# Retention and a gated two-layer network in one kernel: a given TensorE order, held-back weight sums and three releases for the weight slabs

## The chip, the cores and the metric

The kernel runs on one core of a Trainium2 chip. The metric is device time in microseconds, the median of several runs. Lower is better.

## The reference

```python
# q, k, v: (8, 8, 576, 64); w_in: (512, 2048); w_out: (2048, 512)
scores = (q @ k.T) / sqrt(64)
Dmat   = where(rel >= 0, gamma[h] ** rel, 0)      # gamma = 1 - 2 ** (-5 - head)
x      = (scores * Dmat) @ v                      # then (4608, 512): token by all heads
h      = x @ w_in
g      = h * cos(h)
out    = g @ w_out                                # (4608, 512), float32
```

The first part is causal attention with a decay in place of a softmax. The second is a network of two layers on all 4608 tokens, with `h * cos(h)` between them.

## The kernel before

**Tiling.** The tokens are done in nine blocks of 512 (`NTB` is 9), numbered j. A block holds two chunks of 64 positions for four batches. Two streams of two batches each, `x` and `y` in the names, run through 18 chunks: nine for the first four batches, nine for the other four.

**Attention.** The decay is split into a factor on q, a factor on v and a running state, so that a chunk needs only its own keys and the state. `kv_tile` and `q_tile` load k, v and q through SP's queue into `stgk`, `stgv` and `stgq`, and cast or scale them into `natk`, `natv` and `qnat`. In the first tiles ("fast") ScalarE and VectorE do most of this, later GpSimd does. The tiles are then transposed, by TensorE and a copy (`tpe`, `tph`) or by a DMA (`txb`), into `kt` and `qt`. `session` then makes up to four kinds of small products of 64 by 64: q with the old state (L652), q with k (L634), the new state (L643) and, after VectorE has masked the scores into `pt` (L723), the masked scores with v (L661). ScalarE copies the result into `xt` and the state into `sbd`.

**The network.** `mlp1` multiplies `xt` with `win` (L763), four products to a group. ScalarE takes the cosine into `cb` (L771) and VectorE multiplies it into `gt` (L774). For blocks 0 to 2 a group has 256 columns, later 512. The second layer of block 0 is plain (`plain2`, L800). The others use seven products in place of eight (`wino2`, L886). This needs sums of the activations (`s`) and sums of the second weights (`wsums`, L826): six into `tw`, two that overwrite a quarter of `wout`. These overwrites may only run once `plain2` has read that part. ScalarE and VectorE drain the results into `os`, and SP's queue stores them.

**What sets the order.** `graph` lists all tasks with a priority in ns, and `Graph.run` plans them. It keeps a clock for each engine, takes the task that can start first, and among those that can start within some 40 to 60 ns the one with the smallest priority. Each engine runs its tasks in the planned order, and waits on semaphores where a producer or a buffer's last reader isn't done. Buffers come from pools (six PSUM banks `bk`, three `stgk`, three `stgv`, two `stgq` and so on). The planner models instruction fetches: `fetched` keeps a task back while the next block of 256 instructions is not there, with 6000 ns for a fetch and 3500 more for three of them. In its gaps at the start TensorE runs dummy products on a tile of ones (`warm`, L418), so that it isn't idle.

**Weights.** `win` and `wout` come in four slabs of 512 KB each, which GpSimd's queue issues (`load_w`). The first slab is issued once the first v load has landed, and the seven others once the second half of the second tile's q has landed. Two later k loads wait for two slabs of `wout` (`GATE`).

Of the kernel before, what the change touches and what calls it, by code (L numbers as in the profile page):

```python
# [29 lines left out]
class Prog:  # L30
# [9 lines left out]
    def add(self, eng, fn, r=(), w=(), sem=None, after=()):  # L40
# [4 lines left out]
        for k in w:  # L45
            readers = self.rd.get(k, [])
            deps += [d for d in readers if d.eng != eng or d.sem or sem]
            deps += self.wr.get(k, [])
# [54 lines left out]
class Buf:  # L103
    __slots__ = ("pool", "slot", "tasks", "left", "free")

    def __init__(self, pool):
        self.pool, self.slot, self.tasks, self.left, self.free = pool, None, [], 0, 0.0


class Task:  # L110
    @property
    def allocs(self):
# [3 lines left out]
                 "port", "name", "order", "late", "ops", "ni", "pre")  # L116
# [13 lines left out]
def slack(a, b):  # L130

    return Graph.SLACK if b.eng == "pe" and (a.eng == "pool" or a.dma is not None) else 0


class Graph:


    BACKLOG, FETCH, SLOW, MARGIN, SLACK, DX, DLAT = 3500, 6000, 3500, 60, 0, 1.18, 2400

    def __init__(self, pools):  # L140
        self.tasks, self.wr, self.rd = [], {}, {}
        self.pools = {p: [0.0] * n for p, n in pools.items()}
        self.fifo = {p: [] for p in pools if p not in ("bk", "s", "sn", "cb")}
        self.holder = {p: [None] * n for p, n in pools.items()}

    def add(self, eng, dur, parts, prio=None, alloc=(), dma=None, port=False, name="", late=0.0, ni=0):
        t = Task()
        t.ni, t.pre = ni, 0
# [54 lines left out]
    def run(self, dma_rate):  # L203
        self.prios()
        free = {e: 0.0 for e in ("pe", "act", "dve", "pool", "sp")}
        ready = {e: [] for e in free}
        dma_free, port_free = 0.0, {"dve": 0.0, "pool": 0.0}
        est, order, count, got, cold = {}, [], 0, [], True
        for t in self.tasks:
            est[t] = 0.0  # L210
            if not t.wait:
                ready[t.eng].append(t)
# [15 lines left out]
        def fetched(t):  # L228

            k, s = math.ceil(count / 256 - 1.754), 0  # L230
            while k >= 0 and (k + 1.754) * 256 <= count + t.ni + (self.MARGIN if t.ni > 60 else 0):
                if k < len(got):
                    s = max(s, got[k] - t.dur * ((k + 1.754) * 256 - count) / t.ni)
                elif t.ni > 60:
                    s = max(s, free["pe"] + self.FETCH - t.dur)
                k += 1
            return s

        def pick(e):
            cand = []  # L240
            for t in ready[e]:
                a = slots(t)
# [5 lines left out]
                if t.dma is not None and e != "pool":  # L248
                    s = max(s, dma_free - self.BACKLOG)
                if t.ni:  # L250
                    s = max(s, fetched(t))
                cand.append((s, t))
            if e == "pe":
                due = [t for t in ready[e] if all(any(f is not None and f <= free[e] + 1500 for f in self.pools[b.pool])
                                                  for b in t.allocs if b.pool != "bk") and sum(b.pool == "bk" for b in t.allocs) > 2 and t.prio <= free[e] + 300 and est[t] <= free[e] + 1500 and fetched(t) <= free[e] + 500]
                if due:
                    d = min(due, key=lambda t: t.prio)
                    cand = [(s, t) for s, t in cand if t is d or not any(b.pool == "bk" for b in t.allocs)]
                    mine = [s for s, t in cand if t is d]
                    if mine:  # L260
                        cand = [(s, t) for s, t in cand if t is d or s + t.dur <= mine[0] + 150]
# [7 lines left out]
        while n < len(self.tasks):  # L269
# [14 lines left out]
            if e == "pe":  # L284
                if cold and s - free[e] > 300:
                    t.pre = int((s - free[e] - 200) // 75)
                    count += 2 * t.pre
                cold = cold and t.name != "m1_0_0"
                count += 0.53
            free[e] = s + t.dur  # L290
            if t.ni:
                while (len(got) + 0.74) * 256 <= count + t.ni:
                    at = s + t.dur * max(0, (len(got) + 0.74) * 256 - count) / t.ni
                    got.append(at + self.FETCH + (self.SLOW if len(got) in (3, 10, 17) else 0))
                count += t.ni
            if t.port:
                port_free[e] = s + t.dur
            for b in t.allocs:
# [6 lines left out]
                self.holder[b.pool][i] = b  # L305
            done = s + t.dur
            if t.dma is not None:
                dma_free = max(dma_free, s + (2400 if e == "pool" else 1100)) + t.dma * self.DX
                done = dma_free + self.DLAT
# [7 lines left out]
            for o in t.succ:  # L317
                end = next(x for d, x in o.deps if d is t)
                est[o] = max(est[o], (done if t.dma is not None else s + end) + lat(t, o) + slack(t, o))
# [4 lines left out]
        self.end = max(free.values())  # L324
        return self.order


class Kernel:
# [16 lines left out]
    LEAD = 1  # L345
    NOXBAR = set(range(7))
    PERIOD, T0, T1 = 31000, 18000, 30000
# [30 lines left out]
    def build(self):  # L378
        self.graph()
        order = self.G.run(None)  # L380
# [34 lines left out]
    def warm(self, n):  # L415
        def mm(e):
            for _ in range(n):
                inst = e.matmul(ap(self.at(self.wb), 512, 0, 128, 0, [1, 128]), self.ONE.ap(), self.ONE.ap(),  # L418
# [70 lines left out]
    def kv_tile(self, x, gen, R, xbar, fast, gate=()):  # L489
# [14 lines left out]
        def casts():  # L504
# [16 lines left out]
            else:  # L521
                for b2 in range(2):
                    self.tpe(t["natk"], 512 * b2, [(b2,)], 4, t["kt"], 512 * b2, (b2,), "act")
# [14 lines left out]
    def q_tile(self, x, gen, i, xbar, fast, gate=()):  # L538
# [4 lines left out]
        for b2 in range(2):  # L543
            t = {k: Buf(k) for k in ("stgq", "qnat")}
            t["qt"] = Buf("qt" if nr > 1 else "q8")
            self.kv[x, gen, r0 // 2]["stgq"] = t["stgq"]
# [19 lines left out]
            else:  # L566
                self.tpe(t["qnat"], 0, [(y,) for y in range(nx)], 4 * nx, t["qt"], 0, (0,), "dve" if fast else "act")

    def tpe(self, src, off, rk, n, dst, doff, wk, eng):
        bk = Buf("bk")  # L570

        def mm(e):
            tb = self.at(bk).ap().bitcast(BF16)
            for c in range(n):
# [5 lines left out]
                 alloc=() if self.first else (self.wb,), name="tpe")  # L580
# [36 lines left out]
    def session(self, outs, scs, prio):  # L617
# [64 lines left out]
        def part(streams, rk, wk, after=()):  # L682
# [10 lines left out]
            t += 31 * max(map(len, streams))  # L693
# [85 lines left out]
    def store(self, j, half, os, cols=(0, DM)):  # L779
# [3 lines left out]
        for p0, n, gen, r in ([(0, 128, g0, r0)] if one else [(0, 64, g0, r0), (64, 64, g0 + 1, 0)]):  # L783
            at = ((4 * gen + 2 * half) * S + CH * r) * DM + c0
            self.one("sp", 675, lambda e, p0=p0, n=n, at=at: e.dma_start(
                bass.AP(self.out, at, [[DM, n], [S * DM, 2], [1, cn]]),
                ap(self.at(os), 1024, p0, n, c0, [512, 2], [1, cn])),
                r=[(os, c) for c in range(2) if cols[0] <= 256 * c < cols[1]],
                sem=lambda p0=p0: f"o{os.slot}_{p0}_{c0}", dma=1400 * cn / DM * n / 128)
# [21 lines left out]
    def wsums(self):  # L811
# [7 lines left out]
        for q in range(2):  # L819
            k0, k1 = q, 2 + q  # L820
            for dst, x, y, r, w in (
# [5 lines left out]
                         r=r, w=[w], port=True)  # L827

    def wino2(self, j, base, span):
# [25 lines left out]
        A, Bb, C = Buf("bk"), Buf("bk"), Buf("bk")  # L855
# [24 lines left out]
        for n, p in enumerate((1, 2, 6, 5, 7, 3, 4)):  # L880
            l, rr, keys, bank, first = spec[p]
            for q in range(2):
                def mm(e, l=l, rr=rr, bank=bank, first=first, q=q):
                    for f in range(4 * q, 4 * q + 4):
                        for tt in range(2):
                            inst = e.matmul(ap(self.at(bank), 512, 0, 128, 256 * tt, [1, 256]), l(f, tt), rr(f),  # L886
                                            start=(first and f == 0 and tt == 0), stop=True, skip_group_check=True)
                    return inst
                self.one("pe", 8 * 109, mm, ni=16, r=keys(q), w=[(bank,)], prio=base + span * (2 * n + q) / 14, name=f"P{p}_{j}")

            def view(h, c):
# [135 lines left out]
```

## Time and profile before

| quantity | value |
|---|---|
| median of 4 runs | 307.58 us |
| the four runs | 305.73, 306.20, 308.96, 316.32 us |
| the profiled execution | 316.32 us, span 314.6 us |
| mean granted TensorE clock in it | 0.978 |
| data moved | 46.80 MB in 126,397 packets |

The profiled execution is the 316.32 us one, so sums are made against that and then set beside the median.

The page cuts the span into 40 slices of 7.9 us. A digit is the busy share in tenths; the clock's digit is what was granted; the last row is in GB/s.

```profile
PE   8987999799989999999999599999999999999995
DVE  3574972366875658898469367775679767676641
PEclk9999999789979999999999899999999999999999
GB/s 168 222 155 206 206 228 203 252 264 193 218 177 123 156 180 301 156 198 69 228 232 234 218 19 237 83 85 197 163 31 71 69 2 0 99 36 2 52 85 134
```

TensorE is busy nearly everywhere, and the clock dips in a few slices. The groups of instructions (busy us, mean ns of one, idle before them and what ended it) that carry most of it are these:

```profile
L763 PE MATMUL bk<-xt,win 128*128 128x256 bf16 (+1 forms) x768 | 142.6, 332 | 2.2 <-issue 1.3
L774 DVE TENSOR_TENSOR gt<-bk,cb 128x256 bf16<-128x256 f32 (+1 forms) x192 | 103.8, 555 | 62.4 <-ACT cb L771 55.9
L771 ACT ACTIVATE cb<-bk,cpi 128x256 bf16<-128x256 f32 (+1 forms) x192 | 108.6, 584 | 58.3 <-PE bk L763 56.7
L723 DVE TENSOR_TENSOR pt<-bk,tri 128x512 bf16<-128x512 f32 (+1 forms) x46 | 29.6, 683 | 16.9 <-PE st L643 13.7
L886 PE MATMUL bk<-tw,s 128*128 128x256 bf16 x256 | 32.5, 278 | 0.0
```

A matmul's mean is its latency, and matmuls overlap; the spacing of a row in the timeline gives the cost of one. The other groups of L886 on TensorE, with `wout` or `gt`, look alike.

### The profile page before, as it was taken

To read this page: it belongs to the slowest core of one execution; us is meant where nothing else is said; L and a number is where in the kernel's file an instruction comes from. 1 tells how busy PE (TensorE), PEld (TensorE's weight loads), DVE (VectorE), ACT (ScalarE), POOL (GpSimd) and SP (SyncE) were. 2 spreads that over 40 slices of the span, in tenths; PEclk is the share of its full clock that TensorE was granted. 3 is DMA by queue.
4 is the path that set the end of the run, shared out by engine and by line. 5 is a ranking of instruction groups with operands and counts; after the bars stand their busy time and mean duration, and the time that the engine had idled before them with its cause. 6 is when DMAs were issued, how large, how long until landed. Compare 5 with 4: busy or idle time off the path is not lost.

```text
span 314.6 us, 10094 instructions
## 1 busy us (share of the span) xinstructions
PE 298.9 (95%) x4277; PEld 217.2 (69%) x4277; DVE 205.1 (65%) x371; ACT 188.7 (60%) x340; POOL 109.1 (35%) x134
## 2 busy tenths in 40 slices
PE   8987999799989999999999599999999999999995
PEld 8866754688868888656856365668646666666684
DVE  3574972366875658898469367775679767676641
ACT  3376744779849687765375466564686764455430
POOL 2261058749606583751253451312542000000000
PEclk9999999789979999999999899999999999999999
DMA  8999999998974999992999829349821100200123
GB/s 168 222 155 206 206 228 203 252 264 193 218 177 123 156 180 301 156 198 69 228 232 234 218 19 237 83 85 197 163 31 71 69 2 0 99 36 2 52 85 134
DMA packets 126397, 46.80 MB, mean 149 GB/s; under 512 B 105104, under 2 KB 122000, under 8 KB 126352
## 3 DMA queue, kind: packets, MB, share of 16 engines
q1 hardware_dynamic: 122128, 41.95, 62.0%
q0 software_dynamic: 4224, 4.19, 8.3%
q8 instruction: 34, 0.56, 0.8%
q14 instruction: 11, 0.09, 0.1%
HBM read 36.70 MB, written 9.44 MB: 147 GB/s over the span
## 4 chain that ended last, share of the span: by engine, by line
PE 89%; issue 3%; DVE 2%; DMA 2%; POOL 2%; ACT 1%
PE bk L763 40%; PE bk L886 32%; PE bk L800 4%; PE bk L418 2%; PE bk L652 2%; PE bk L661 2%; DMA stgq<-in_q_dram 2%; PE bk L634 2%; PE bk L575 2%; PE st L643 2%; PE bk L593 1%; DVE gt L774 1%; POOL win L743 1%; POOL wout L747 1%; DVE pt L723 0%
## 5 line engine op out<-in xcount | busy, mean ns | idle before, releaser
L763 PE MATMUL bk<-xt,win 128*128 128x256 bf16 (+1 forms) x768 | 142.6, 332 | 2.2 <-issue 1.3
L774 DVE TENSOR_TENSOR gt<-bk,cb 128x256 bf16<-128x256 f32 (+1 forms) x192 | 103.8, 555 | 62.4 <-ACT cb L771 55.9
L771 ACT ACTIVATE cb<-bk,cpi 128x256 bf16<-128x256 f32 (+1 forms) x192 | 108.6, 584 | 58.3 <-PE bk L763 56.7
L763 PEld LDWEIGHTS bk<-xt,win 128*128 128x128 bf16 x768 | 73.8, 99 | 45.3 <-issue 2.4
L512 POOL TENSOR_TENSOR natv<-stgv,wv 128x512 bf16<-128x512 f32 x38 | 41.6, 1107 | 35.4 <-DMA stgv<-in_v_dram 23.1
L477 POOL CAST natk<-stgk 128x512 bf16<-128x512 f32 x36 | 22.2, 630 | 65.6 <-DMA stgk<-in_k_dram 36.7
L557 POOL TENSOR_TENSOR qnat<-stgq,wq 128x512 bf16<-128x512 f32 x36 | 38.5, 1087 | 14.2 <-DMA stgq<-in_q_dram 8.2
L723 DVE TENSOR_TENSOR pt<-bk,tri 128x512 bf16<-128x512 f32 (+1 forms) x46 | 29.6, 683 | 16.9 <-PE st L643 13.7
L476 ACT ACTIVATE sbd<-st 128x512 bf16<-128x512 f32 x32 | 19.3, 602 | 23.0 <-PE st L643 23.0
L886 PE MATMUL bk<-tw,s 128*128 128x256 bf16 x256 | 32.5, 278 | 0.0
L886 PE MATMUL bk<-wout,s 128*128 128x256 bf16 x256 | 32.3, 273 | 0.0
L886 PE MATMUL bk<-wout,gt 128*128 128x256 bf16 x256 | 31.6, 273 | 0.0
L886 PEld LDWEIGHTS bk<-tw,s 128*128 128x128 bf16 x256 | 25.2, 100 | 6.0
L886 PEld LDWEIGHTS bk<-wout,s 128*128 128x128 bf16 x256 | 24.6, 98 | 6.7
L886 PEld LDWEIGHTS bk<-wout,gt 128*128 128x128 bf16 x256 | 24.6, 98 | 4.7 <-DVE pt L723 0.2
L476 ACT ACTIVATE sn<-bk 128x512 f32<-128x512 f32 x24 | 14.5, 605 | 19.0 <-PE bk L886 19.0
L476 ACT ACTIVATE xt<-bk 128x512 bf16<-128x512 f32 x36 | 23.0, 693 | 0.3 <-PE bk L661 0.2
L898 DVE TENSOR_TENSOR os<-bk,sn 128x512 f32<-128x512 f32 x24 | 16.4, 684 | 8.3 <-PE bk L886 8.2
L886 PE MATMUL bk<-tw,gt 128*128 128x256 bf16 x128 | 17.3, 282 | 0.0
L418 PE MATMUL bk<-one 128*128 128x128 bf16 x181 | 14.8, 249 | 1.1 <-DVE lq L441 1.1
L886 PEld LDWEIGHTS bk<-tw,gt 128*128 128x128 bf16 x128 | 12.8, 101 | 4.1 <-issue 0.3
L643 PE MATMUL st<-natv,natk 64*64 64x64 bf16 x512 | 11.8, 196 | 3.8 <-issue 3.8
(63 smaller groups left out, 235.8 us busy)
## 6 DMA issues: line engine op xcount, KB each, us to landing
stgk<-in_k_dram SPq DMA_DIRECT2D x32, 256.0 KB, 5.1
stgv<-in_v_dram SPq DMA_DIRECT2D x32, 256.0 KB, 5.4
out_dram<-os SPq DMA_DIRECT2D x15, 512.0 KB, 3.7
stgq<-in_q_dram SPq DMA_DIRECT2D x12, 512.0 KB, 5.9
stgq<-in_q_dram SPq DMA_DIRECT2D x8, 256.0 KB, 5.0
win<-in_moe_w_in_dram POOLq DMA_DIRECT2D x4, 512.0 KB, 7.7
wout<-in_moe_w_out_dram POOLq DMA_DIRECT2D x4, 512.0 KB, 14.7
out_dram<-os SPq DMA_DIRECT2D x6, 256.0 KB, 3.5
```

The source lines that it names most:

```text
L418: inst = e.matmul(ap(self.at(self.wb), 512, 0, 128, 0, [1, 128]), self.ONE.ap(), self.ONE.ap(), start=True, stop=True, skip_group_check=True)
L476: return self.one(eng, dur, lambda e: e.activation(dst(), src(), AF.Copy), r=r, w=w, **kw)
L477: return self.one(eng, dur, lambda e: e.tensor_copy(dst(), src()), r=r, w=w, port=True, **kw)
L512: self.one(ve, vd, lambda e, b2=b2: e.tensor_tensor(ap(self.at(t["natv"]), 1024, 0, 128, 512 * b2, [D, H], [1, D]), ap(self.at(t["stgv"]), ...
L557: self.one("dve" if fast else "pool", 620 if fast else 990, lambda e, t=t, y=y: e.tensor_tensor(ap(self.at(t["qnat"]), 1024, 0, 128, y * 5 ...
L643: yield lambda e, b2=b2, c=c, o=o: e.matmul(ap(self.ST[u[0]], 512, 64 * ph, 64, (4 * b2 + c) * 64, [1, 64]), ap(self.at(self.keys(u)["natk ...
L723: self.one("dve", 610, lambda e, hp=hp: e.tensor_tensor(ap(self.at(pt), 1024, p0, n, 512 * hp, [64, 8], [1, 64]), ap(self.at(sc[hp]), 512, ...
L763: inst = e.matmul(ap(self.at(bk), 512, 0, 128, 0, [1, n]), ap(self.WIN, 4 * DFF, 0, 128, c * DFF + 128 * f, [1, 128]), ap(self.at(xt), 204 ...
L771: self.one("act", 70 + n, lambda e: e.activation(ap(self.at(cb), TB, 0, 128, 0, [1, n]), ap(self.at(bk), 512, 0, 128, 0, [1, n]), AF.Sin, ...
L774: self.one("dve", 75 + n / 0.96, lambda e: e.tensor_tensor(ap(self.at(gt), NF * TB, 0, 128, f * TB + 256 * h0, [1, n]), ap(self.at(bk), 51 ...
L886: inst = e.matmul(ap(self.at(bank), 512, 0, 128, 256 * tt, [1, 256]), l(f, tt), rr(f), start=(first and f == 0 and tt == 0), stop=True, sk ...
L898: self.one("dve", 610, lambda e: e.tensor_tensor(view(h, c), ap(self.at(bank), 512, 0, 128, 0, [256, 2], [1, 256]), ap(self.at(sn[name]), ...
```

## The change

1. **TensorE's order is given.** `run` takes a list of 388 task numbers and lets TensorE take only the next of them. The planner's fetch model and its rule for tasks that are due are removed. The first twelve tasks of SP's queue keep the order in which `graph` lists them. The planner's picture of the DMA queues becomes a class of its own.
2. **Sums of the second weights.** The tasks of `wsums` are named "T", and the planner lets none of them start before 48,000 ns of its own clock.
3. **Weight slabs.** Slab 0 of `win` waits for the first half of the first tile's v, the second slab for the first half of the second tile's q, and all six others for the first half of its v.
4. **Dummies.** They have 512 columns, not 128, and `fill` counts how many go into each gap ahead of the first product with `win`.
5. **The last block.** The last of the seven products is split by token half into two banks, with a drain and a store for each half.
6. **Waits.** A writer now waits for readers on its own engine too, except on TensorE.
7. A form of `mlp1` with seven products is added for blocks from `SEVEN` on. `SEVEN` is 10 and the blocks are 0 to 8. `NOXBAR` gains chunk 7. Base times of the priorities change (`PERIOD`, `T0`, `T1`).

```diff
-            deps += [d for d in readers if d.eng != eng or d.sem or sem]
+            deps += [d for d in readers if d.eng != "pe" or eng != "pe"]
...
-    BACKLOG, FETCH, SLOW, MARGIN, SLACK, DX, DLAT = 3500, 6000, 3500, 60, 0, 1.18, 2400
+    BACKLOG, DX, DLAT, HOLD, START, LEAD, TSUMS = 3500, 1.18, 2400, 0, 800.0, 12, 48000.0
...
+class Queues:
+    def __init__(self):
+        self.sp, self.pool, self.held = 800.0, 0.0, []
+    def end(self, eng, at, dur):
+        if eng == "pool":
+            a = max(self.pool, at + 3000)
+            self.pool = a + dur
+            self.held.append((a, a + dur))
+            return self.pool
+        t = max(self.sp, at + 1100)
...
-    def run(self, dma_rate):
+    def run(self, given):
         self.prios()
+        turn = iter(given)
+        first = next(turn)
+        lead = [t for t in self.tasks if t.eng == "sp"][:self.LEAD]
...
-            est[t] = 0.0
+            est[t] = self.TSUMS if t.name == "T" else 0.0
...
-        def fetched(t):
...
             for t in ready[e]:
+                if e == "pe" and t.idx != first or e == "sp" and lead and t is not lead[0]:
+                    continue
...
+    def fill(self):
...
+            if t.eng == "pe":
+                at = max(free["pe"], 1150.0)
+                gap = s - at - 100
+                slow = max(0.0, min(gap, 4500 - at))
+                t.pre = max(0, int(slow / 440 + (gap - slow) / 220)) if gap > 150 else 0
...
-    NOXBAR = set(range(7))
-    PERIOD, T0, T1 = 31000, 18000, 30000
+    SEVEN = 10
+    ORDER = [int(x) for x in """3 2 1 0 4 5 6 9 7 8 15 17 10 14 16 18 11 21 19 12 13 23 22 41 40 35 25 26 32 30 31 27 45 24 20 29 33 92
...
+    FIRST = [(0, "v", 0), (1, "q", 0), (1, "v", 0)]
+    NOXBAR = set(range(8))
+    PERIOD, T0, T1 = 27000, 19000, 29000
...
-                inst = e.matmul(ap(self.at(self.wb), 512, 0, 128, 0, [1, 128]), self.ONE.ap(), self.ONE.ap(),
+                inst = e.matmul(self.at(self.wb).ap(), self.ONE.ap(), ap(self.ONE, 128, 0, 128, 0, [0, 4], [1, 128]),
...
                 self.one("dve", 610, lambda e, dst=dst, x=x, y=y: e.tensor_tensor(dst(), x(), y(), ALU.subtract),
-                         r=r, w=[w], port=True)
+                         r=r, w=[w], port=True, name="T")
...
-        A, Bb, C = Buf("bk"), Buf("bk"), Buf("bk")
+        last = j == NTB - 1
+        A, Bb, C = [Buf("bk") for _ in range(1 + last)], [Buf("bk")], [Buf("bk")]
...
+            final = last and p == 4
...
+                    for f in range(8) if final else range(4 * q, 4 * q + 4):
+                        for tt in (q,) if final else range(2):
...
-        gate = [(self.kv[1, 0, 0]["stgq"],)]
-        for s, x in enumerate((0, 2, 1, 3)):
-            self.load_w("win", x, gate if s >= self.LEAD else [(self.kv[0, 0, 0]["stgv"], 0)], 100 + s)
-        for s in range(4):
-            self.load_w("wout", s, gate, 200 + s)
+        for s, x in enumerate((0, 2, 1, 3, 4, 5, 6, 7)):
+            x1, n, b2 = self.FIRST[min(s, len(self.FIRST) - 1)]
+            t = self.kv[x1, 0, 0]
+            gate = [(t["stgq", b2],) if n == "q" else (t["stg" + n], b2)]
+            self.load_w("win" if s < 4 else "wout", x % 4, gate, 100 + s)
```

In the order of each engine this comes to the following. On VectorE both q casts of the first tile now stand ahead of the first transposed copy, and the sums into `tw` and `wout` stand behind the 31st of block 0's 32 products into `gt`, ahead of the masks of the next session (one of them between its first and second masks). On GpSimd four slabs and not six stand ahead of the second tile's `natv`, and the second slab has a release of its own. On TensorE the first products with `win` start before the second tile's scores, products of `plain2` stand between and after the next sessions, and the last products with `win` are followed by 136 of `wino2` and not 120.

## The prediction

> **What bounds the kernel now.** I read the page's busy times first, then the chain of waits, then what TensorE waited for, then the timeline around each wait.
>
> ```profile
> PE 298.9 (95%) x4277; PEld 217.2 (69%) x4277; DVE 205.1 (65%) x371; ACT 188.7 (60%) x340; POOL 109.1 (35%) x134
> PE 89%; issue 3%; DVE 2%; DMA 2%; POOL 2%; ACT 1%
> ```
>
> TensorE is the bound from its first real product to its last: 95% busy, 89% of the chain, and nobody else is over 65%. A change can gain only what TensorE loses to idling and to a slow clock. The waits of TensorE (us in total, times, longest):
>
> ```profile
> PE st L643 <- issue: 3.8, 1, 3.8
> PE bk L634 <- POOL natv L512: 1.7, 1, 1.7
> PE bk L763 <- issue: 1.3, 1, 1.3
> PE bk L575 <- issue: 1.2, 1, 1.2
> ...
> PE bk L763 <- ACT xt L476: 0.8, 1, 0.8
> PE bk L634 <- ACT qt L476: 0.7, 1, 0.7
> ```
>
> The three "issue" waits, 6.3 us together, lie inside one group of equal instructions with no semaphore between them. In the timeline (start, duration):
>
> ```profile
> 172.42 0.44 PE L643 MATMUL st<-natv,natk 64*64 64x64 bf16 x29
> 176.69 0.22 PE L643 MATMUL st<-natv,natk 64*64 64x64 bf16 x3 [3.83 <-issue]
> ```
>
> 29 of 32 run, then nothing for 3.83 us. That is a late instruction fetch. Counting two instructions for each matmul and one for each extra wait, the three stalls stand at blocks 3.76, 9.75 and 20.76 of 256 instructions, each 1.2 to 1.5 us after a 16,384-byte packet of the instruction queue ends (28.54, 87.01, 175.26 us in the trace). So block k is needed at k + 0.754 and, by where the packets start, asked for about one block earlier. From asking to use took 2 to 10 us (8.9, 7.3 and 10.3 for the three late ones). Where TensorE runs attention, 256 instructions last only a few us.
>
> The clock adds to this (stretch, busy of PE, PEld, DVE, ACT, POOL, then clock, DMA):
>
> ```profile
> 55.00:62.00 7.00, 5.27 (x146) 4.41 (x147) 2.58 (x4) 5.00 (x11) 5.29 (x8) 0.73 1.26 252
> 86.00:92.00 6.00, 4.63 (x88) 3.38 (x76) 4.25 (x9) 3.63 (x8) 0.00 (x0) 0.75 0.97 237
> ```
>
> The clock record is at half rate for 6.8 us from 58.3, 3.4 us from 89.0 and 3.4 us from 177.8, each after a stretch in which TensorE mostly idled or ran small tiles. At most half of 13.6 us is lost, 6.8 us.
>
> At the start, POOL works through its queue in order:
>
> ```profile
> 18.36 2.29 POOL L743 DMA_DIRECT2D win<-in_moe_w_in_dram  x3 [7.03 <-DMA stgq<-in_q_dram]
> 20.62 2.25 POOL L747 DMA_DIRECT2D wout<-in_moe_w_out_dram  x3
> 22.84 1.10 POOL L512 TENSOR_TENSOR natv<-stgv,wv 128x512 bf16<-128x512 f32 x1
> ```
>
> Three slabs wait for a q load, six slabs are issued, and only then comes the natv that TensorE waits for (1.75 us, to 24.09).
>
> **What the Trainium skill says.** "Runtime: NRT & Kernel Launch", Instruction fetch mechanics: instructions come in 16 KiB blocks of 256 while the current ones run, and the cost of a block's edge is mostly hidden. The block agrees (34 packets, 0.56 MB); "hidden" does not in this trace, 6.3 us. "TensorE: Matmul & The Clock Gate", What's actually happening: half clock after an idle window of about 3.4 us, the windows free-running. The trace agrees, its stretches are 3.4 and 6.8 us. The same page, Back-to-back issue gap: N / 2.4 + 2.5 ns, so 216 ns for 512 columns; the trace's L800 x4 take 0.86 us, 215 each. "SBUF — State Buffer", Who interferes with whom: VectorE and GpSimd lock each other out of a shared port; the two sums into wout took 0.69 and 1.28 us, which fits and doesn't prove it.
>
> **The change part by part.** The same matmuls remain on TensorE; only 181 dummies of 128 columns become 47 of 512. At 56 and 216 ns both are 10.1 us, and the 268 instructions fewer move every later position back by one block. From the first win product on, both have the same work: 290.9 us (20.43 to 311.35) less 10.2 idle and 6.8 clock, some 274. The seven-product form of the first layer is never reached (SEVEN is 10, there are 9 blocks), and NOXBAR changes no count (64 + 64 transposes on TensorE, 8 + 8 by DMA in both orders): nothing for both, as nothing runs. The own-engine waits for readers cost nothing: 61 waits of VectorE on itself against 66.
>
> *Start.* The profiled kernel's second q load of the second tile is issued at 12.0, because its buffer waits for a cast that stands behind a copy which waits for a transpose; SP's v loads queue behind it (12.51). In the new VectorE order both casts come first, at about 7.3 and 8.0. I estimate that q is issued near 9.7 and v near 10.8, which at the 5.4 us median of these loads lands near 16. Slabs 3 to 8 then start there and not at 18.36, and natv, now after four issues of 0.76 and not six, ends near 20.3 and not 23.9. The new slab 2 waits for the first q half (near 14) and lands near 21.7 at the 7.7 us median of these slabs (19.5 at their shortest, 5.5); product 17 waits for it. Then 12 products (1.3), scores (0.25), two attention sessions (2.3 us in the trace with their mask waits) and 13 products (1.4) put product 41 near 27.0 (24.8), against 30.4 now. But the fetch of block 2 is asked for at about 21.5 in the weight traffic and needed right there; at 4.8 to 8.9 us (its neighbours now) it comes at 26.3 to 30.4. Gain 0 to 4.1, I take **-2.5**.
>
> *Sums held back.* Eight sums move from between gt products to behind the 31st of 32, just ahead of the masks of the next session. Behind them in VectorE's queue stand those masks (L723, 0.65 each), and TensorE's intra products wait for them. Two sums overwrite wout and must wait for the last reads of it by the plain product. From the end of that read: 0.2 + 0.69 to 1.28 for the second overwrite, one tw sum 0.68, two masks 1.3: 2.9 to 3.5 us. TensorE has about 2.1 of other work in its new order there. So the mask wait is 0.8 to 1.4 us (0.27 now), and another up to 1.0 in the second session. Against that, the qt wait (0.73) and the xt wait (0.75) go, since plain products now stand after the qt copies and after the session. Net -1.2 to +0.9, I take **-0.7**. The stretch without large products shrinks from 6.1 us (54.3 to 60.4) to 3 to 4.4, so one of the two half-clock windows should go: 0 to -3.4, I take **-1.7**.
>
> *Order for fetches.* With the rows' durations (16 small products in 0.25 us alone, 128 in 1.05 in a paired session) the work between asking and needing is 5.0, 5.7 and 6.3 us at the three late blocks now. 268 instructions fewer make the edges of one block later fall near the same work. Listed in the new order, the start has 3.2 there (counted above), the place of the stall at 87 us 3.2 and that of 172.7 us 5.5. So I find no more room than now at these places, and other short blocks of 4.1 to 5.1 us between about 55 and 110 us, with perhaps 1 us of waits on top. What speaks for few stalls is the other runs: the profiled execution is 7.4 to 10.6 us over the other three, about what its late fetches cost. Stall and clock window at 172.7 make 3.83 + 1.7, at 87.1 1.16 + 1.7: 8.4 together. I count them as absent from a common execution of either kernel (0 to **-8.4**, I take -8.4) and add for the shorter blocks: each may stall 0 to 1.5 us and bring a half-clock window of 1.7, so 0 to +6.4 for two of them. I take **+1.0**, a third of one.
>
> *End.* The last product is split into two banks, each drained by 256 columns and stored alone. The 0.60 us copy becomes about 0.35, and the last store halves: 0 to -0.5, I take **-0.4**. SP has one store more, behind nothing.
>
> *Sum.* The profiled execution took 316.3 us (span 314.6, 1.7 around it): 316.3 - 2.5 - 0.7 - 1.7 - 8.4 + 1.0 - 0.4 = **303.6**. It is the slowest of four; the median is 307.58 and the fastest 305.73. The kernel before without its three late fetches is 316.3 - 8.4 - 1.3 = 306.6, in line with those. So the sum is 1.3% under the median.
>
> **The rivals.**
> - *Short blocks arrive late (slower).* If fetches take 7 us or more where the new order leaves 3 to 5, two blocks stall with their windows (+6.4), the start gains nothing, the masks cost +0.5 net and both old clock windows stay: 316.3 - 8.4 + 0.5 + 6.4 - 0.4 = 314.4. One such block (311.2) already passes the 1%. For it: three fetches took over 7 us in this trace, amid 189 to 292 GB/s. Against: half of them took under 4.7, and most runs are much shorter than this one.
> - *The waits change places (no change).* Slab 2 and its neighbours hold product 17 and the masks hold the session: start -1.0, masks +0.5, no window won, short blocks +0.6: 316.3 - 1.0 + 0.5 - 8.4 + 0.6 - 0.4 = 307.6. For it: wout slabs took 11.8 to 16.6 us to land. The change then does not do what it says, since the sums are still ahead of the masks.
> - *Everything fits.* Start -4.1, masks -1.2, both windows -3.4, no new stall: 316.3 - 4.1 - 1.2 - 3.4 - 8.4 - 0.4 = 298.8. Against: it needs the 4.8 us fetch amid the weights.
>
> **How the numbers follow.** My sum 0.41 (300.6 to 305.6 by itself), everything fits 0.16, no change 0.25, slower 0.18. One per cent of 307.58 is what a measurement here can tell: under 304.5 is faster, over 310.7 slower. Faster: 0.16 and most of 0.41, 0.51; slower 0.18; the rest 0.31. The range 298.5 to 309 takes in all but the slow case.
>
> **What would show it.** Right: product 41 before 29 us; no TensorE wait on ACT just before and after the second block's attention; at most one half-clock stretch in 55 to 65; no group cut by an issue wait near 170. Wrong: issue waits inside groups near 25, 55, 70, 90 or 170 us; L723's masks (now L762) holding TensorE for over 1.5 us; a wait for win at product 17 of over 4 us.

## The result and the profile after

The changed kernel takes **315.51 us** (median of 12 runs, 313.45 to 319.12). The kernel before took 312.1 in the 17 runs taken so far, the first four among them, 305.73 to 316.32. The ratio is 1.0261, 95% interval 1.021 to 1.0312: slower. It compares only the executions within 1.5% of each kernel's fastest; medians in this text are over all runs. The forecast was 303.6, with a range to 309.

The profiled execution took 317.7 us, span 315.9. Its page has the same bound as before (busy times; granted clock in 40 slices; shares of the chain of waits):

```profile
PE 296.3 (94%) x4143; PEld 207.1 (66%) x4143; DVE 208.1 (66%) x372; ACT 190.3 (60%) x343; POOL 110.7 (35%) x134
PEclk9999999999979999999999799999999999999999
PE 84%; DMA 6%; DVE 4%; issue 4%; ACT 1%; SPq 1%; DVEq 0%; ACTq 0%
```

TensorE is still 94% busy and no other engine is nearer to being the bound. So what can be lost is again idle time and half clock on TensorE. Its waits (us in total, times, longest):

```profile
PE bk L614 <- issue: 3.2, 1, 3.2
PE bk L700 <- issue: 2.8, 1, 2.8
PE bk L614 <- DVE qnat L596: 1.7, 1, 1.7
PE st L682 <- issue: 1.3, 1, 1.3
PE bk L457 <- DVE lq L480: 1.1, 1, 1.1
PE bk L700 <- DVE pt L762: 1.1, 2, 0.8
PE bk L802 <- issue: 1.0, 1, 1.0
...
PE bk L802 <- DMA win<-in_moe_w_in_dram: 0.6, 1, 0.6
```

Four "issue" waits, 8.3 us, have taken the place of the three of before. The timeline of TensorE shows the two long ones (start, duration, idle before):

```profile
85.87 0.34 PE L614 MATMUL bk<-idn,natk 128*128 128x128 bf16 x3
89.42 0.27 PE L614 MATMUL bk<-idn,natk 128*128 128x128 bf16 x1 [3.20 <-issue]
...
173.70 0.24 PE L700 MATMUL bk<-pt,natv 64*64 64x64 bf16 x5
176.76 0.41 PE L700 MATMUL bk<-pt,natv 64*64 64x64 bf16 x27 [2.82 <-issue]
```

Three of four transposes run, then nothing for 3.2 us; five of 32 small products, then nothing for 2.8. By the count of instructions (two for each product, one for each extra wait) these stand at blocks 8.75 and 19.76, and the shorter two (1.5 us near 69, 1.3 near 29, between one start and the next) at 6.75 and 2.75. The prediction listed 3.2 us of work between asking and needing at the start (block 2) and at the place of the stall at 87 us (block 8), 5.5 at that of 172.7 (block 19 now), and 4.1 to 5.1 for others, block 6 (4.9) among them. The places were right; what they cost was not. The clock fell to half for 3.4 us from 89.4 and for 3.4 us from 178.2, just after the long ones. The half-clock stretch of before at 58 to 65 is gone (busy of PE, PEld, DVE, ACT, POOL, then clock, DMA share, GB/s):

```profile
55.00:62.00 7.00, 6.11 (x110) 4.96 (x104) 3.74 (x8) 6.26 (x14) 6.66 (x8) 1.00 1.10 253
85.00:92.00 7.00, 3.80 (x80) 2.92 (x81) 4.11 (x6) 2.77 (x5) 2.49 (x2) 0.82 1.05 217
```

### The profile page after: what moved, and what is told of

The parts are those of the page before. It is cut to its first block, busy times and chain, and to the rows that moved or that the text cites. A ratio compares the mean times of both kernels' runs of the same rounds, so it can differ in the third digit from the quotient of the medians.

```text
span 315.9 us, 9834 instructions
## 1 busy us (share of the span) xinstructions
PE 296.3 (94%) x4143; PEld 207.1 (66%) x4143; DVE 208.1 (66%) x372; ACT 190.3 (60%) x343; POOL 110.7 (35%) x134
## 4 chain that ended last, share of the span: by engine, by line
PE 84%; DMA 6%; DVE 4%; issue 4%; ACT 1%; SPq 1%; DVEq 0%; ACTq 0%
PE bk L802 39%; PE bk L1060 31%; PE bk L972 4%; DMA win<-in_moe_w_in_dram 3%; PE bk L673 2%; PE bk L700 2%; DVE pt L762 2%; PE bk L691 2%; DMA stgq<-in_q_dram 2%; DMA stgv<-in_v_dram 2%; PE st L682 1%; DVE gt L813 1%; PE bk L614 1%; PE bk L632 1%; SPq L589 1%
## 5 line engine op out<-in xcount | busy, mean ns | idle before, releaser
L813 DVE TENSOR_TENSOR gt<-bk,cb 128x256 bf16<-128x256 f32 (+1 forms) x192 | 105.2, 557 | 72.9 <-ACT cb L810 66.8
L802 PE MATMUL bk<-xt,win 128*128 128x256 bf16 (+1 forms) x768 | 138.9, 330 | 2.4 <-issue 1.0
L516 POOL CAST natk<-stgk 128x512 bf16<-128x512 f32 x36 | 23.9, 685 | 67.2 <-PE st L682 31.0
L515 ACT ACTIVATE sn<-bk 128x512 f32<-128x512 f32 (+1 forms) x26 | 14.5, 567 | 21.9 <-PE bk L1060 21.8
L1079 DVE TENSOR_TENSOR os<-bk,sn 128x512 f32<-128x512 f32 (+1 forms) x25 | 16.6, 664 | 11.2 <-PE bk L1060 11.1
L1060 PE MATMUL bk<-tw,gt 128*128 128x256 bf16 x128 | 16.3, 273 | 0.0
L972 PE MATMUL bk<-wout,gt 128*128 128x512 bf16 x64 | 15.6, 379 | 0.0
L515 ACT ACTIVATE kt<-bk 128x512 bf16<-128x512 bf16 x20 | 11.8, 595 | 6.2 <-PE bk L614 5.9
L700 PE MATMUL bk<-pt,natv 64*64 64x64 bf16 x576 | 11.2, 194 | 4.0 <-issue 2.8
```

The lines of the kernel that those rows point to most:

```text
L515: return self.one(eng, dur, lambda e: e.activation(dst(), src(), AF.Copy), r=r, w=w, **kw)
L516: return self.one(eng, dur, lambda e: e.tensor_copy(dst(), src()), r=r, w=w, port=True, **kw)
L700: yield lambda e, b2=b2, c=c: e.matmul(ap(self.at(ob[u]), 512, 64 * hp, 64, (4 * b2 + c) * 64, [1, 64]), ap(self.at(self.keys(u)["natv"]), ...
L802: inst = e.matmul(ap(self.at(bk), 512, 0, 128, 0, [1, n]), ap(self.WIN, 4 * DFF, 0, 128, c * DFF + 128 * f, [1, 128]), ap(self.at(xt), 204 ...
L813: self.one("dve", 75 + n / 0.96, lambda e: e.tensor_tensor(ap(self.at(gt), NF * TB, 0, 128, f * TB + 256 * h0, [1, n]), ap(self.at(bk), 51 ...
L972: inst = e.matmul(self.at(bk).ap(), ap(self.at(gt), NF * TB, 0, 128, f * TB + 256 * half + 128 * tt, [1, 128]), ap(self.WOUT, NF * DM, 0, ...
```

## One account for all runs

For each profile I sum the gaps of over 0.3 us from one product's start to the next, less the usual spacing, at a block edge (positions k + 0.725 to k + 0.775). These are the "edge stalls", good to 0.2 us. I also take the time at half clock before TensorE's last product, of which at most half is lost. "Useful work" below is the sum of the usual spacings of all products issued so far, without dummies. A block is taken as asked for when the block before it is first needed, an estimate. The runs are described in the next part.

| kernel | median, us | profiled | edge stalls | half clock | rest |
|---|---|---|---|---|---|
| before | 312.1 | 316.3 | 7.7 | 13.7 | 301.8 |
| before again | | 305.3 | 1.1 | 0 | 304.2 |
| after | 315.5 | 317.7 | 9.1 | 6.8 | 305.1 |
| half a block | 315.3 | 314.1 | 6.3 | 6.8 | 304.4 |
| before's order | 310.8 | 309.6 | 5.3 | 0 | 304.2 |
| sums early | 315.4 | 317.1 | 8.4 | 10.2 | 303.6 |
| old releases | 319.8 | 320.8 | 7.4 | 10.2 | 308.3 |
| early edges | 318.2 | 316.1 | 6.7 | 10.2 | 304.3 |
| late edges | 312.6 | 310.8 | 5.3 | 0 | 305.4 |
| both edges | 316.7 | 314.5 | 5.3 | 6.8 | 305.9 |
| before's order, best edges | 308.0 | 311.4 | 3.3 | 10.2 | 303.0 |
| new order, better edges | 312.9 | 313.9 | 6.2 | 6.8 | 304.4 |
| before's order, bad edges | 312.3 | 312.8 | 6.5 | 6.8 | 302.8 |
| after, light loads | 307.6 | 306.3 | 2.1 | 0 | 304.2 |
| before, light loads | 305.3 | 306.0 | 2.0 | 3.4 | 302.3 |

Rest = profiled time - edge stalls - half of the half-clock time. Executions from 305 to 318 us have a rest of 302 to 306, in both orders; only the old releases stand out. Without them the rest averages 303.1 in the old order (six profiles) and 304.7 in the new (eight). So some 1.6 us of the loss may lie outside the block edges; since half of the half-clock time is an upper bound, this is rough.

The medians come from several sessions: runs 1 to 4, 5 to 8, 9 to 11, and 12 and 13. In these the kernel before took 309.5, 309.2, 311.4 and 309.4 us, against 312.1 in the session of the changed kernel. A difference of medians across sessions is therefore uncertain by 2 to 3 us. The ratios in brackets set a run against the kernel before in the run's own session.

## The experiments

Theories: *late fetches* (blocks with little work between asking and needing stall TensorE); *held-back sums*; *slab releases*; *the order's own waits* for buffers and producers.

**1. Half a block.** Dummies of 512 columns are cut in four, so all block edges move.

```diff
+    fine = 21
...
+        fine = min(n, self.fine)
+        self.fine -= fine
...
-            for _ in range(n):
...
+            for i in range(n):
+                for c in range(4 if i < fine else 1):
+                    w = 128 if i < fine else 512
```

> The changed kernel, with its first 21 dummy products of 512 columns each made as four of 128: the same dummy time, 126 instructions more ahead of everything else, so every later block edge falls half a block earlier in the work. Nothing else is changed. By the work between asking and needing there are then eleven blocks with under 4 us of work (1.6 to 3.8), against two now (3.2, 3.2). Theory 'late fetches': each of these stalls by some 1 to 4 us, 10 to 30 us in all less the 9 of now, so 321 to 335 us, with TensorE waits on issue inside groups at block positions k + 0.754. Theories 'held-back sums', 'slab releases' and 'the order's own waits for buffers and producers': nothing that they speak of moves, 314 to 317 us.

315.27 us (ratio to before 1.0183, 1.0084 to 1.0282): as slow as the change and within the rivals' range, so a clear miss for the number of late fetches. But the stalls moved: those at 86 and 174 are gone, and small ones stand elsewhere, 2.1 us at 110 and 0.3 to 1.2 us at six more. The waits of this run:

```profile
PE bk L1067 <- issue: 2.2, 3, 0.9
PE bk L707 <- issue: 1.9, 1, 1.9
```

The three short blocks that stalled after 195 us waited 0.8 to 1.2 us each, since their packets ended 1.4 to 3.1 us after asking. Short blocks alone do not price a stall; the length of the fetch at that place counts as much.

**2. The order of before in the changed kernel** (ORDER replaced, `fine` = 2).

> The changed kernel with the list of task numbers of the kernel before (same tasks, TensorE's order as before), and two of the dummies cut in four, which puts the block edges to within some 10 instructions of where they fell before. Slab releases, held-back sums, 512-column dummies and the split end stay. Theory 'late fetches': the blocks have again the work between asking and needing that they had before (shortest 4.2 and 4.5 us, not 3.2), so 306 to 310 us. Theory 'the order's own waits': also 306 to 310. Theories 'held-back sums' and 'slab releases': the loss stays, 313 to 317.

310.79 us (1.0101, 1.0073 to 1.013), just above the range of the first two theories, which this run does not tell apart. TensorE's order, with its edges, carries about 1.6 of the 2.6% that the change loses. The releases, held-back sums and split end together bring no gain with the old order.

**3. and 4. Sums early; old releases.**

```diff
-    BACKLOG, DX, DLAT, HOLD, START, LEAD, TSUMS = 3500, 1.18, 2400, 0, 800.0, 12, 48000.0
+    BACKLOG, DX, DLAT, HOLD, START, LEAD, TSUMS = 3500, 1.18, 2400, 0, 800.0, 12, 0.0
```

> The changed kernel with the sums of the second weights not held back (the planner may start them from 0 and not from 48,000 ns); TensorE's order is the same list, and its instructions shift by 7. Theory 'held-back sums': the waits for masks go and the time falls to 311 to 313 us. Theory 'late fetches': the block edges stay where they are, so 314 to 317, or a little more if gt products now come later.

315.43 us (1.0186, 1.0081 to 1.0292; four runs): no change that four runs can show. Holding the sums back is worth nothing measurable either way.

```diff
-    FIRST = [(0, "v", 0), (1, "q", 0), (1, "v", 0)]
+    FIRST = [(0, "v", 0), (1, "q", 1)]
```

> The changed kernel with the slab releases of the kernel before: slab 0 by the first half of v, all seven others by the second half of the second tile's q. TensorE's order and its instruction count stay. Theory 'slab releases': the start is where the loss is, 311 to 313 us. Theory 'late fetches': 314 to 317 us, since the same blocks are short of work (3.2 us at 6 and at 55 us of useful work).

319.82 us (1.03, 1.0185 to 1.0416; four runs): by its median slower than expected by either theory, with no sign of a gain. The new order starts `win` products earlier and, with the old releases, waits 2.7 us for a slab where the changed kernel waits 0.6. So the new releases are not the loss.

**5. to 7. Edges moved in part of the kernel only.** First-layer products are cut in pieces of fewer columns, which adds instructions in one place and gives them back to a full block in another.

```diff
+            i, self.m1 = self.m1, self.m1 + 1
+            parts = next((p for a, b, p in self.CUT if a <= i < b), 1)
             for c in range(4):
-                inst = e.matmul(
+                for p in range(parts):
+                    w = n // parts
+                    inst = e.matmul(
```

> The changed kernel with the block edges moved only in its first third: 16 dummies cut in four (96 instructions more), and then first-layer products of 256 columns cut in two between 56 and 94 us of useful work until exactly 256 instructions are added, so that every edge after that falls where it did in the changed kernel. The blocks of 3.2 and 4.9 us of work at 55 and 41 us become 7.0 and 7.7; a few of 2.7 to 4.7 us arise at 58 to 77, where fetches were quicker. Theory 'late fetches': the stalls at 69 and 86 us and the half-clock stretch at 89 go (1.5 + 3.4 + 1.7), some 1 to 3 us of small ones come, and the stall near 174 stays: 310 to 313 us. Theory 'the order's own waits for buffers and producers': the order is untouched, 315 to 317.

318.19 us (four runs, 311.92 to 321.82): not the gain expected. The stalls at 69 and 86 are gone, but a block asked for at 107 us, with 3.6 us of work, got its packet's end 6.3 us after asking, where the profiles before it had 2.4 to 5.0: 3.8 us idle and 6.8 us at half clock.

> The changed kernel with the block edges moved only between 105 and 155 us of useful work: 14 first-layer products cut into two or four pieces, 128 instructions more at 105 and 128 more at 154, so that edges before and after fall where they did. The block asked for at 131 us (5.5 us of work) goes; those in its place are asked for at 119 and 123. Theory 'late fetches': the stall near 174 us (3.0) and the half-clock stretch at 178 (1.7) go, and those at 69 and 86 stay: 310 to 312 us. Theory 'the order's own waits': 315 to 317.

312.63 us (20 runs; 1.0133, 1.0092 to 1.0174, below the interval of the change): just above the range, but 1.3% gained (2.9 us by the medians) with the order, buffers and releases untouched. Where the changed kernel stood still for 2.8 us, TensorE now runs through:

```profile
170.50 0.47 PE L683 MATMUL st<-natv,natk 64*64 64x64 bf16 x32
170.78 0.45 PE L701 MATMUL bk<-pt,natv 64*64 64x64 bf16 x32
171.70 2.75 PE L807 MATMUL bk<-xt,win 128*128 128x512 bf16 x12 [0.47 <-ACT sbd L516]
```

From 135 to 140 us of useful work it loses well under 1 us where the changed kernel loses about 5, stall and half clock together. It is the clearest sign that a late fetch, and not the order's own waits, cost the time there.

> Both movements of edges together in the changed kernel, 512 instructions more, order, buffers, sums and releases untouched. Theory 'late fetches': the two gains add up, 306 to 309 us, level with the kernel before. Theory 'the order's own waits': 315 to 317.

316.72 us (312.01 to 319.48): the late stall is gone again and the one near 112 is there again (3.5 us, and half clock for 3.4 us after it). So 5 and 7 fail by the same block.

**8. The kernel before once more.**

> The kernel before once more, for a profile of another execution. Theory 'late fetches': what one execution loses at its block edges differs, and an execution of 306 to 309 us lacks most of the 7.7 us of edge stalls and of the 13.6 us at half clock of the profiled 316.3, in particular the 3.8 us at 172. If instead it shows the same stalls and clock and is shorter elsewhere, counting them as absent was wrong.

305.28 us, with 1.1 us of edge stalls and no half clock before the end. So these two executions of one kernel differ by their fetches and the half clock after them. Its waits hold no issue line at all; these are the longest:

```profile
PE bk L575 <- DVE qnat L557: 1.6, 3, 1.3
PE bk L634 <- DVE gt L774: 1.4, 1, 1.4
PE bk L418 <- DVE lq L441: 1.1, 1, 1.1
```

Its 32-product groups near 165 us are whole: the fetch that took 9 us from asking to its packet's end in the first profile took 3.6 here, at the same edge and with the DMA engines as busy.

**9. to 11. Edges chosen by the fetch times seen so far.**

> The changed kernel with the TensorE order of the kernel before, 32 dummies cut in four (192 instructions more ahead of everything) and 14 first-layer products of 256 columns cut in two (11 between 13 and 35 us of useful work, 3 at 84 to 87; 112 instructions). By the fetch times seen at each place in the ten profiles so far, the block edges then fall where they cost least, about half of what they cost with this order before (an estimate of 6.8 us against 12.0 for the second run of this study). Theory 'late fetches': 304 to 308 us, below both kernels or level with the one before. If the order and the rest of the change alone decide: 310 to 312, as in that run.

307.99 us (22 runs, 305.09 to 311.37; before in the same session 311.41, up to 315.21). Ratio 1.0021, 0.9991 to 1.0051, against 1.0101 for the same order in run 2: the intervals lie apart, so the edges alone are worth some 0.8%. It is the only kernel of the study that does all the work and is level with the kernel before. Its median is lower because the executions over 312 are missing, but the ratio doesn't show it faster.

> The changed kernel with its own order, 14 dummies cut in four (84 instructions) and 13 first-layer products cut at 104 to 113 and 147 to 170 us of useful work, edges chosen in the same way (estimate 8.8 us of edge cost, against 17.8 for the changed kernel and 16.4 for the run with late edges moved). One block of 2.3 us is left, asked for at 80. Theory 'late fetches': 307 to 311 us, 5 or more below the changed kernel, so that the order itself costs at most 2. Theory 'the order's own waits': 314 to 317, or at best the 312 to 313 of the run with late edges moved.

312.93 us (four runs; 1.0156, 1.0092 to 1.022): 2.6 better than the change by the medians, not the 5 expected, and the intervals of the two just touch. The block left at 80 us of work stalled 2.5 us, with a half-clock stretch, and one at 26 us 2.3.

> The changed kernel with the TensorE order of the kernel before and 30 dummies cut in four (180 instructions more), nothing else: a shift that puts nine block edges where less than 3.7 us of work lies between asking and needing. Theory 'late fetches': an estimate of 24.9 us of edge cost against 12.0 for the second run, which this estimate is likely to overstate as it did for the half-block shift: 316 to 322 us. Theory 'the order's own waits': the order and buffers are those of the second run, 309 to 312.

312.33 us (310.4 to 318.08): a miss; only 1.5 us over run 2, which the rival's range nearly holds. One of the nine short blocks stalled over 2 us, one 2.0; the others lost nothing or up to 0.9 us.

**12. and 13. The edges left alone, the DMA's load taken away.** Loads of k, v and q bring two heads of eight once a buffer has been filled.

```diff
+    def heads_of(self, *key):
+        seen = self.__dict__.setdefault("filled", set())
+        old = key in seen
+        seen.add(key)
+        return 2 if old else H
...
-                    ap(self.at(t[name]), 1024, p0, n, 512 * b2, [D, H], [1, D]),
-                    bass.AP(self.src[src], at, [[D, n], [S * D, H], [1, D]])),
+                    *(lambda h: (ap(self.at(t[name]), 1024, p0, n, 512 * b2, [D, h], [1, D]),
+                                 bass.AP(self.src[src], at, [[D, n], [S * D, h], [1, D]])))(self.heads_of(name, t[name].slot, b2))),
```

> The changed kernel in which every load of k, v and q into a buffer that has been filled once brings two of the eight heads and not all eight (it leaves out three quarters of those loads, and the other heads' inputs are those of an earlier tile). Every instruction of TensorE, its order, the block edges and all waits stay. Theory 'late fetches by a busy DMA': the fetches near 63, 80 and 170 us land within 1 to 4 us, the stalls at 69 and 86 shrink (their blocks still have only 4.9 and 3.2 us of work, so up to 1 us each may stay) and that at 174 goes with both half-clock stretches: 306 to 310 us. If a fetch takes its time whatever the DMA does, or the order's own waits set the time: 314 to 317.

307.64 us (20 runs; 0.9978, 0.9952 to 1.0004): 7.9 us under the changed kernel by the medians, 2.8% by the ratios, with the same TensorE program to the instruction. Lighter loads also bring the inputs sooner, but that is little of it: of the 11.4 us between the two profiles 7.0 are edge stalls, 3.4 half clock, and 0.9 the rest. The stretches ahead of the three late fetches, first in the changed kernel, then here (last columns: clock, DMA share, GB/s):

```profile
165.00:174.00 9.00, 8.94 (x146) 5.16 (x144) 6.45 (x10) 6.17 (x11) 1.85 (x2) 1.00 1.06 243
77.00:86.00 9.00, 8.20 (x169) 7.29 (x167) 7.66 (x16) 7.38 (x15) 8.51 (x10) 1.00 1.20 228
64.00:70.00 6.00, 5.41 (x129) 4.58 (x127) 4.73 (x11) 4.63 (x9) 2.38 (x5) 1.00 1.16 269
```

```profile
160.00:166.00 6.00, 5.91 (x131) 3.59 (x128) 4.09 (x7) 3.87 (x7) 0.00 (x0) 1.00 0.16 45
76.00:82.00 6.00, 5.19 (x139) 4.48 (x136) 6.00 (x10) 4.92 (x10) 6.00 (x7) 1.00 0.09 19
60.00:66.00 6.00, 5.99 (x138) 5.18 (x140) 5.30 (x13) 4.31 (x11) 1.99 (x4) 1.00 0.41 95
```

With the DMA engines 10 to 40% busy and not over 100%, the block with 3.2 us of work (asked for at 76) has its packet's end some 3.5 us after asking, not 7, and the stalls at 69 and 86 are gone. That at 174 shrinks from 3.0 to 1.6.

> The kernel before with the same cut in its loads. Theory 'late fetches by a busy DMA': it loses the executions of 311 to 316 us and stays at 304 to 307, with edge stalls of under 2 us in all. If the difference between executions has another cause: the same spread, 306 to 315.

305.26 us (13 runs, 304.88 to 306.88): the spread of 8.4 us that the kernel before has with full loads on the same chip (306.39 to 314.83) is gone. So the DMA's load makes most of the late fetches late, in both kernels. Whether the wait is in the engines' queues or in the memory behind them, these runs don't separate.

All fifteen profiles say the same of single fetches. I took those asked for in the first 245 us and the share of the DMA engines in the 3 us after asking. With a share under 0.5 the packet ended over 5 us after asking in 2 of 113 cases (median 2.1 us). With a share over 0.9 it did so in 52 of 211 (median 3.8). Busy engines make a late fetch likelier; most fetches come in time even then.

Between the two light-load kernels 2.4 us remain, which the change costs apart from busy traffic; one late fetch is part of them. By TensorE's progress in the two profiles the new order gains about 4 us from 34 to 42 us of useful work (a half-clock stretch of the old order's run lies in it), and loses about 2 at 54 to 62, 1 to 2 at 76 to 82, 1.6 at 135 to 140 (the remaining late fetch) and 0.7 at 220 to 240.

## Why the prediction was wrong

- **What bounds it, and which blocks would be short:** right. Blocks 2, 6, 8 and 19, of 3.2, 4.9, 3.2 and 5.5 us, are the four that stalled. The length of the work alone did not pick them: block 11, asked for near 104 us with little over 4 us of work, ran through, as its packet ended less than 1 us after asking.
- **The step that failed: -8.4 with +1.0.** The late fetches of the profiled execution were counted "as absent from a common execution of either kernel", and two short blocks were priced at "a third of one". For the kernel before, some executions do lack them (run 8). For the changed kernel none was seen to: of its 12 executions the fastest took 313.45 us, and all three profiles in which both the new order's edges and its loads are untouched (after, sums early, old releases) have the stalls near 69, 86 to 88 and 173 to 177, 7.4 to 9.1 us of edge stalls in all, and 6.8 to 10.2 us at half clock. Of the 14.5 us that the profiled execution before lost at edges and half clock (7.7 and half of 13.7), the sum took off 8.4 and 1.7 and added 1.0, so it left 5.4. The changed kernel's profile has 9.1 + 3.4 = 12.5. That is 7.1 of the 14.1 us between forecast and profile. I had a block of 3.2 us of work at the place where the old order had just stalled, with 237 to 252 GB/s moving in the windows shown, and took a low value from a wide bound instead of asking whether that fetch could land in 3 us there. In the changed kernel's profile the packets of blocks 2, 6, 8 and 19 end 5 to 7 us after asking.
- **The other half, 6.9 us,** lies in the rest. The sum took it from 301.8 to 298.2 (-2.5, -0.7, -0.4), and it came to 305.1. Two executions of the kernel before already differ by 2.4 there (301.8 and 304.2), so the start from one profile was low. The gain taken at the start, below, did not last, and with light loads the new order shows small losses elsewhere (run 13).
- **Start, -2.5:** product 41 starts at 28.76, before the 29 named, but the second execution of the kernel before has it at 28.77. The gain was over one execution, and it did not last: after product 42 stands the block 2 stall, which came as feared (1.3 us). Product 43 starts at 30.18, 0.3 before the 30.50 of the profiled execution before and 1.2 after the 28.98 of the second. The q and v loads were issued earlier, near the times estimated, and landed no sooner, with about 200 GB/s moving in the first 20 us: slabs 3 and 4 left at 19.62, not at 16, and natv ended at 24.0, not 20.3.

```profile
19.62 1.48 POOL L782 DMA_DIRECT2D win<-in_moe_w_in_dram  x2 [4.74 <-DMA stgv<-in_v_dram]
21.08 1.50 POOL L786 DMA_DIRECT2D wout<-in_moe_w_out_dram  x2
22.98 1.04 POOL L551 TENSOR_TENSOR natv<-stgv,wv 128x512 bf16<-128x512 f32 x1 [0.40 <-DMA stgv<-in_v_dram]
```

- **Second block's attention, -0.7 and -1.7:** between 34 and 42 us of useful work TensorE gains 4.1 us on the profiled execution, more than the 2.4 of the sum. Against the second execution of before, which has no half-clock stretch there, it gains 1.2. The qt wait is gone; an xt wait of 0.7 stands later, at 107. The masks hold TensorE 0.8 us in that session, within the bound, and holding the sums back is worth nothing measurable by itself (run 3).
- **End, -0.4:** right by the traces. From the last product's start to the end of the span 3.5 us became 3.1, and the last copy takes 0.38 us, not 0.60.
- **The rival that came true** is "Short blocks arrive late": 314.4 against 315.5 measured. Two long stalls with a half-clock stretch each are its mechanism (3.4 + 1.7 + 3.0 + 1.7 = 9.8 us, where it had 6.4). That its sum comes so near is in part luck: it had 3.4 too little here, and it kept the 3.4 us of the old half-clock stretch at 58 to 65, which is gone. The evidence against it, "half of them took under 4.7", mixed places with idle and with busy DMA engines.

Still open: why the same fetch took 9 us in one execution of the kernel before and 3.6 in another, with DMA engines as busy in both. What lies ahead of it in the same engine's queue may decide it; no view shows that.

## What to carry to other kernels

Where an engine runs many tiny instructions, list for each block of instructions the work between asking and needing beside the DMA load at that moment. In this kernel a short block in busy traffic could stall for microseconds, often with a half-clock stretch after it; in quiet traffic it was mostly free, with one stall of 1.6 us. Look at such blocks one by one and not by an average, but don't trust a price taken from earlier runs: in runs 1, 5, 10 and 11 such prices were off by several microseconds. Take at least two profiles of the kernel before, or a disturbance of one execution will be booked as the gain of a change. A reordering of a program this dense has to be judged with its block edges, and easing the DMA at the critical fetches can be worth more than an order, as it was here.

## What the hardware showed

- The Trainium skill's page "Runtime: NRT & Kernel Launch", Instruction fetch mechanics, calls the cost of a block's edge mostly hidden. With light loads that nearly holds (about 2 us in 33 or 34 blocks); with full loads it was 1.1 to 9.1 us in this study.
- A stall brought half clock in some cases and not in others: 2.1 us at 110 did (run 1), 2.7 us at 123 (run 2) and 2.0 at 86 (run 6) did not, so a stall's length alone doesn't decide it. The prediction took half clock to follow an idle window of about 3.4 us. The stretches last 3.4 us or twice that, but the idle gaps ahead of them were shorter: 3.2 and 2.8 in the changed kernel, 1.2 at 87 in the kernel before.
- In run 12, with the DMA engines nearly idle from 161.3 us, one packet still began 4.9 us after the estimated asking, at 165.0. What lets a fetch start is thus not just traffic, or the estimate of when it is asked for (one block ahead) is off there. It is off at other places: the packet of the changed kernel's block 29 ends at 252.5, 1.5 us before its estimated asking.
